# Fewer, larger transfers for x and for the remainders, and the tail product first, in a fused attention and gMLP kernel

## The chip, the cores and the metric

The kernel runs on one core of a Trainium2 chip. The time is device time in microseconds; five runs of the kernel before gave 479.23 to 485.28, with a median of 483.63. A profile is one further reading of such an execution with the hardware profiler on: it lists every instruction with its start, its duration and the engine that it ran on.

## The reference

For 8 batches of 8 heads, with 576 rows of 64 numbers each, the kernel computes an attention in which scores more than `tau` below their row's maximum are dropped, and feeds the joined heads to a gated MLP that mixes rows.

```python
scores = 0.125 * (q @ k.T)                       # per head, 576 x 576
scores = where(scores >= max(scores) - tau, scores, -1e9)
attn = softmax(scores);  x = join_heads(attn @ v)          # 576 x 512 per batch
h = relu(x @ w_in);  u, v = h[:, :512], h[:, 512:]
v_n = (v - mean(v)) / sqrt(var(v) + 1e-6)
out = (u * (w_spatial @ v_n + b_spatial)) @ w_out
```

Inputs and outputs are fp32.

## The kernel before

**Tiling.** Two heads form a pair; there are 32 pairs, four to a batch. A head has 576 rows, that is four blocks of 128 and a remainder of 64. The remainder rows of the two heads of a pair, and of two neighbouring pairs, are put together so that they fill 128 partitions. One *step* computes the scores of one block of one pair for both heads: 128 rows by 2 x 576 columns in fp32. An even pair has four steps (blocks c = 0 to 3). An odd pair has five: first c = 4, the remainder rows of both pairs, and then c = 0 to 3. So there are 144 steps, 18 for each batch. This document calls them s0 to s17:

| steps | pair of the batch | blocks |
|---|---|---|
| s0 to s3 | first | 0, 1, 2, 3 |
| s4 to s8 | second | 4, 0, 1, 2, 3 |
| s9 to s12 | third | 0, 1, 2, 3 |
| s13 to s17 | fourth | 4, 0, 1, 2, 3 |

**One step** (`step`, L606). `scores` (L563) gives the product of q and k in two parts. The first 512 columns of both heads are four independent 64 x 64 products, two heads by two halves of the rows, here called the quadrants (L576). The last 64 columns of both heads are one product over all 128 partitions with a block-diagonal matrix `kd`, here called the tail (L580). The result goes to a PSUM tile of three banks, `s`, of which there are two; a step therefore waits until ScalarE has read the scores of two steps ago. VectorE takes the row maximum (L618). ScalarE computes exponentials from the scores (L641), and VectorE masks them one step later (L599); for blocks 2 and 4 ScalarE does the masking too (L635, L637) and VectorE only shifts the maximum (L622). After the mask of every second block SP issues a DMA transpose of 18 blocks of 128 x 128 (`pT`, L603), or of nine for the remainder rows (`ptr`, L594).

**Jobs.** While VectorE and ScalarE work on a step's scores, PE does up to three jobs that are given out by a list written by hand. In a step, jobs whose result ScalarE takes out of PSUM come first, then those of VectorE; `pv_rest` is last. All jobs share two PSUM banks in turn, so that a job waits until the bank of the job before the last has been read.

- `qk_main` and `qk_rem` (L238, L256) transpose q and k of the next pair in blocks 0, 1 and 2; ScalarE copies them out (L251, L264, L253), and POOL makes `kd` from the copy (L269).
- `pv` (L309) multiplies the transposed weights by v for two blocks of a pair; VectorE divides by the row sums (L302, L304) and writes `xn`. It runs at s3, s4, s7, s8, s12, s13, s16 and s17. The weights used at s4 and s13 belong to the pair before the last.
- `pv_rest` (L336) does the same for the remainder rows of two pairs and writes `xr`. It runs in block 1 of an odd pair, at s6 and s15.
- the gMLP of the batch before: four kinds of jobs, `moe_v`, `moe_u`, `moe_s` and `moe_o`, one in almost every step from step 26 on. `moe_v` begins at s8 of the cycle after the batch.

**x transposed.** The gMLP needs x transposed, `xT`. For most pairs SP issues a DMA transpose of the pair's four blocks as soon as the last are divided (L331), and another of one block for each two pairs' remainders (L352). For pairs 0 to 6, 30 and 31 PE transposes them (`x_pe`, L365), because the list says so.

**Loads.** `load` (L102) brings q, k and v of two pairs at a time, with three main transfers of 512 KB and four smaller ones for the remainder rows: q's and k's go to a fifth block of the tile for q, v's to a fifth block of v's tile, and the odd heads' remainders of v once more to the upper partitions of a tile of their own, `vx`. POOL brings q, k (L137) and v (L157, L161) into the order that PE needs; q's copy carries the fifth block along. One load is issued per step, in the order of a queue. All DMAs but a few at the start and the end are issued by SP, in order, after the transpose of the step's mask. A DMA that writes to a buffer waits on SP until the buffer is free, and everything behind it waits too.

The program below shows the functions that the diff touches.

Of the kernel before, what the change touches and what calls it, by code (L numbers as in the profile page):

```python
# [17 lines left out]
def kernel(  # L18
# [17 lines left out]
    nc = tc.nc  # L36
# [34 lines left out]
    v_ring = [const.tile([P, 11, D + 1], BF16, name=f"v{i}") for i in range(4)]  # L71
    vn_ring = [const.tile([P, 5, 512], BF16, name=f"vn{i}") for i in range(2)]
    ld_ring = [[const.tile([P, 4, n, D], F32, name=f"{t}{i}")
                for t, n in (("ql", 5), ("kl", 4), ("vl", 5))] for i in range(2)]
    vx_ring = [const.tile([P, 2, D], F32, name=f"vx{i}") for i in range(2)]
# [3 lines left out]
    def clear():  # L79
        nc.vector.memset(kd_ring[0], 0.0)  # L80
        nc.gpsimd.memset(ld_ring[0][2][64:128, :, 4, :], 0.0)
        for t in vx_ring:
            nc.gpsimd.memset(t[0:64], 0.0)
        nc.gpsimd.memset(kd_ring[1], 0.0)
        nc.gpsimd.memset(ld_ring[1][2][64:128, :, 4, :], 0.0)
        for t in v_ring:
            nc.vector.memset(t[:, :, D:D + 1], 1.0)
            nc.vector.memset(t[64:128, 4, D:D + 1], 0.0)
            nc.vector.memset(t[0:64, 5, D:D + 1], 0.0)
            nc.vector.memset(t[64:128, 10, D:D + 1], 0.0)  # L90
        for t in vn_ring:
            nc.vector.memset(t[64:128, 4, :], 1.0)
# [9 lines left out]
    def load(i, n, w, eng=nc.sync):  # L102

        b, hp = divmod(i, HP)
        t = ld_ring[i // 2 % 2][w][:, 2 * (i % 2):2 * (i % 2) + 2 * n]
        src = (q, k, v)[w][b, 2 * hp:2 * hp + 2 * n]

        def main():
            eng.dma_start(
                out=t[:, :, 0:4, :],  # L110
                in_=src[:, 0:512, :].rearrange("h (p c) d -> p h (c d)", c=4))

        def rest():

            u = ld_ring[i // 2 % 2][(0, 0, 2)[w]][(slice(0, 64), slice(64, 128), slice(0, 64))[w]]
            eng.dma_start(out=u[:, 2 * (i % 2):2 * (i % 2) + 2 * n, 4, :],
                          in_=src[:, 512:576, :].rearrange("h p d -> p h d"))

        def rest_b():
            nc.sync.dma_start(  # L120
                out=vx_ring[i // 2 % 2][64:128],
                in_=src.rearrange("(j h) s d -> h s j d", h=2)[1, 512:576])
        return [main, rest] + ([rest_b] if w == 2 else [])
# [7 lines left out]
    def shape_qk(i):  # L131

        ts = []
        for w, nm in enumerate(("qn", "kn")):
            n = 5 - w
            t = qkn.tile([P, n, 2, D], F32, name=nm)
# [6 lines left out]
    def shape_first():  # L143

        qn = qkn.tile([P, 5, 2, D], F32, name="qn")
        kn = qkn.tile([P, 4, 2, D], F32, name="kn")
        for to, t, c, copy in ((qn, 0, slice(0, 4), nc.vector.tensor_copy),
                               (kn, 1, slice(0, 4), nc.scalar.copy),
                               (qn, 0, slice(4, 5), nc.gpsimd.tensor_copy)):
            copy(out=to[:, c], in_=ld_ring[0][t][:, 0:2, c].rearrange("p h c d -> p c h d"))  # L150
        nat[0] = [t.rearrange("p c h d -> p c (h d)") for t in (qn, kn)]

    def shape_v(i):
# [5 lines left out]
                        [v_ring[i % 4].ap[0], [6 * (D + 1), 2], [D + 1, 5], [1, D]]),  # L159
            in_=ld_ring[i // 2 % 2][2][:, 2 * j:2 * j + 2])  # L160
        nc.gpsimd.tensor_copy(out=v_ring[i % 4][:, 5, 0:D], in_=vx_ring[i // 2 % 2][:, j, :])  # L161
# [74 lines left out]
    x_on_pe = [j for _, j in x_jobs] + [NPAIR - 2, NPAIR - 1]  # L236

# [18 lines left out]
    def qk_rem(i):  # L256
        hold = {}

        def mm():
            t = hold["t"] = bank()  # L260
            nc.tensor.transpose(out=t[:, 0:P], in_=nat[i][0][:, 4, :], identity=identf)
# [10 lines left out]
    def first():  # L272
# [3 lines left out]
        for t, w, c, at in ([(ts[0], 0, c, c * P) for c in range(5)]  # L276
                            + [(ts[1], 1, c, c * P) for c in range(4)]):
            nc.tensor.transpose(out=t[:, at:at + P], in_=nat[0][w][:, c, :], identity=identf)
# [30 lines left out]
    def pv(i, part):  # L309
# [9 lines left out]
        def ev():  # L319
            if part == 0:  # L320
                xns[i] = xp.tile([P, 4, P], BF16, name="xn")
            xn = xns[i]
            divide(hold["t"], [(slice(0, P), 0, 4,
                                xn[:, 2 * part:2 * part + 2, :].rearrange(
                                    "p c (h d) -> p (c h) d", h=2))])
            if part == 1:
                if hp == 0:
                    xts[b] = xtp.tile([P, 4, 640], BF16, name="xT")
                if i in x_on_pe:
                    return  # L330
                sends.append(lambda: nc.sync.dma_start_transpose(  # L331
                    out=xts[b][:, hp, 0:512].rearrange("p (c s) -> p c s", s=P),
                    in_=xn.rearrange("p c d -> p (c d)")))
        return "dve", mm, ev

    def pv_rest(m):  # L336

        b, hp = divmod(2 * m, HP)
# [7 lines left out]
        def ev():  # L346
            xn = xns["rest", m] = xp.tile([P, P], BF16, name="xr")
# [3 lines left out]
            if 2 * m + 1 < NPAIR - 1:  # L351
                sends.append(lambda: nc.sync.dma_start_transpose(  # L352
                    out=xts[b][:, hp, 512:640], in_=xn))
        return "dve", mm, ev

    def rest_of(b, f):

        return xts[b][:, f - f % 2, 512 + 64 * (f % 2):576 + 64 * (f % 2)]

    def x_pe(i, rest=False):  # L360
# [4 lines left out]
        def mm():  # L365
            t = hold["t"] = bank16()
            for c in range(4):
                nc.tensor.transpose(out=t[:, c * P:(c + 1) * P], in_=xns[i][:, c, :],
                                    identity=identb)
            if rest:  # L370
                nc.tensor.transpose(out=t[:, 512:640], in_=xns["rest", i // 2], identity=identb)

        def ev():
            if not rest:
                nc.scalar.copy(out=xts[b][:, hp, 0:512], in_=hold["t"][:, 0:512])
                return
            nc.scalar.copy(out=xts[b][:, hp, 0:256], in_=hold["t"][:, 0:256])
            nc.vector.tensor_copy(out=xts[b][:, hp, 256:512], in_=hold["t"][:, 256:512])
            nc.vector.tensor_copy(out=xts[b][:, hp - 1, 512:640], in_=hold["t"][:, 512:640])
# [47 lines left out]
    def moe_v(b, c):  # L427
        hold = {}

        def mm():  # L430
# [4 lines left out]
            for f in range(4):  # L435
                nc.tensor.matmul(out=t, lhsT=xts[b][:, f, c * P:(c + 1) * P],  # L436
# [34 lines left out]
    def moe_u(b, f):  # L471
        hold = {}

        def mm():
            t = hold["t"] = bank()
            for m in range(4):
                if f < 4:
                    nc.tensor.matmul(out=t, lhsT=w_in[:, m, f * P:(f + 1) * P],  # L478
                                     rhs=xts[b][:, m, 0:512], start=(m == 0), stop=(m == 3))
# [83 lines left out]
    def scores(i, c):  # L563
# [8 lines left out]
        else:  # L572
            who = tails = [(i - 1 + k, slice(512, 576), halves[k]) for k in range(2)]
        for h in range(2):
# [4 lines left out]
        for n, m, rows in tails:  # L579
            nc.tensor.matmul(out=view(s[rows], 512, [[448, 2], [1, 64]]), lhsT=qks[n][:, 0, m],  # L580
                             rhs=kd_ring[n % 2], start=True, stop=True)
# [84 lines left out]
    def last_gmlp(b):  # L666

        xt, vn = xts[b], vn_ring[b % 2]
# [3 lines left out]
        for c in range(5):  # L672
            t = bank()
            for f in range(4 if c < 4 else 0):
                nc.tensor.matmul(out=t, lhsT=xt[:, f, c * P:(c + 1) * P],
# [130 lines left out]
    with tc.manual_schedule():  # L806
        for w in (0, 1):
            for f in load(0, 1, w, (nc.sync, nc.scalar)[w]):
                f()
# [6 lines left out]
        for w in (0, 1):  # L816
            for f in load(1, 1, w):
                f()
        for f in load(0, 2, 2):
            f()  # L820
# [9 lines left out]
        for g, (i, c) in enumerate(steps):  # L830
# [4 lines left out]
            if c == 0 and i % 2 and i + 3 < NPAIR or g == 0:  # L835
                for w in range(3):
                    queue.extend(load(i + (3 if g else 2), 2, w))
# [81 lines left out]
```

## Time and profile before

| | |
|---|---|
| median of five runs | 483.63 us |
| lowest, highest | 479.23, 485.28 us |
| profiled execution: device time | 484.91 us |
| its span, first to last instruction | 483.1 us |
| mean granted TensorE clock | 0.992 |
| VectorE, row maximum (L618): 144 of | 1.353 us |
| VectorE, mask (L599): 91 of | 1.474 us |
| SP, transposes issued: pT, xT from xn, xT from xr, ptr | 64, 23, 15, 13 |
| SP, instructions | 272 |
| DMA engines busy, 0 to 115, 115 to 430, 430 to 483 us | 0.90, 0.95, 0.48 |

In the profile "PE" is the matmul stream and "PEld" the loading of weights, which may run beside it. Every fp32 matmul of the program appears as two[...]. In a row of a group or of the timeline, `out<-in` are the program's tiles; in brackets stands how long the engine was idle before, and what ended that. The chain of work that ended last is followed back from the last instruction, at each step to what released it. "SPq" is the time for which SP's queue was held by issuing a DMA, not the time of the transfer; "landing" is when the transfer's completion was seen.

### The profile page before, as it was taken

How to read it: one execution, taken by the hardware profiler on the slowest of the kernel's cores; microseconds unless marked ns; L12 is line 12 of the kernel's file. 1: busy time of each engine (PE TensorE's matmuls, PEld its weight loads, DVE VectorE, ACT ScalarE, POOL GpSimd, SP SyncE). 2: the span in 40 equal slices, each digit the busy share in tenths (PEclk: the TensorE clock that was granted, in tenths of full speed). 3: DMA queues.
4: the chain of work that ended last, by engine and by line, in shares of the span. 5: the costliest groups of instructions: out<-in, count | busy, mean ns of one | idle time of the engine just before them, and what ended most of it. 6: DMA issues, size and time to landing. Idle time of an engine off the chain costs nothing.

```text
span 483.1 us, 10876 instructions
## 1 busy us (share of the span) xinstructions
PE 446.1 (92%) x4153; PEld 226.8 (47%) x4203; DVE 412.8 (85%) x563; ACT 390.8 (81%) x677; POOL 227.2 (47%) x403
## 2 busy tenths in 40 slices
PE   8788888889899999999999999999997999999995
PEld 5244444444544445454544545454543445445542
DVE  3889898989889997999889998999986898899573
ACT  3889998999879798888979798788978689797351
POOL 3453335795438553574427643575416444153021
PEclk9899999999999999999999999999999999999999
DMA  8879899969999899899999899899999989568523
GB/s 231 218 176 202 196 211 206 223 142 190 196 193 187 166 216 224 204 157 191 217 215 173 178 193 229 189 187 188 182 178 199 187 163 211 133 114 125 148 81 116
DMA packets 226131, 88.55 MB, mean 183 GB/s; under 512 B 196896, under 2 KB 221600, under 8 KB 226080
## 3 DMA queue, kind: packets, MB, share of 16 engines
q1 hardware_dynamic: 225424, 86.98, 87.7%
q8 instruction: 33, 0.54, 0.5%
q0 software_dynamic: 160, 0.52, 0.3%
q10 hardware_dynamic: 496, 0.36, 0.2%
q14 instruction: 18, 0.15, 0.1%
HBM read 33.31 MB, written 9.44 MB: 88 GB/s over the span
## 4 chain that ended last, share of the span: by engine, by line
PE 47%; DVE 24%; ACT 20%; issue 6%; DMA 2%; POOL 0%; POOLq 0%; ACTq 0%; DVEq 0%
PE s L576 14%; DVE negm L618 11%; DVE p L599 8%; PE s L580 6%; ACT e L641 5%; ACT e L635 5%; PE f L295 4%; PE f L478 3%; PE f L246 3%; PE f L537 2%; ACT p L637 2%; DMA pT<-p 2%; PE f L508 2%; PE f L290 2%; ACT vrel L446 2%
## 5 line engine op out<-in xcount | busy, mean ns | idle before, releaser
L618 DVE TENSOR_REDUCE negm<-s 128x2 f32<-128x1152 f32 x144 | 194.9, 1353 | 33.2 <-PE s L580 31.7
L576 PE MATMUL s<-qkT 64*64 64x512 f32 x1152 | 159.5, 624 | 14.3 <-ACT e L641 8.3
L599 DVE SCALAR_TENSOR_TENSOR p<-e,ctau 128x1152 bf16<-128x1152 f32 x91 | 134.1, 1474 | 1.2 <-ACT e L641 1.2
L641 ACT ACTIVATE e<-s,negm 128x576 f32<-128x576 f32 x182 | 124.9, 741 | 7.2 <-DVE negm L618 6.7
L580 PEld LDWEIGHTS s<-kd,qkT 128*128 128x128 f32 (+1 forms) x320 | 41.7, 179 | 119.2 <-issue 107.0
L635 ACT ACTIVATE e<-s,negm 128x576 f32<-128x576 f32 x106 | 72.9, 742 | 16.2 <-DVE negm L622 10.9
L269 POOL COPY kd<-qkT 64x64 f32<-64x64 f32 x62 | 26.9, 434 | 101.8 <-ACT qkT L264 100.0
L580 PE MATMUL s<-kd,qkT 128*128 128x128 f32 (+1 forms) x320 | 70.2, 323 | 0.0
L576 PEld LDWEIGHTS s<-qkT 64*64 64x64 f32 x1152 | 30.2, 132 | 46.8 <-ACT e L641 18.3
L454 POOL TENSOR_SCALAR nmean<-sm 128x1 f32<-128x1 f32 (+1 forms) x35 | 16.6, 473 | 71.2 <-ACT vrel L446 59.5
L295 PEld LDWEIGHTS <-pT 128*128 128x128 bf16 x1024 | 41.8, 97 | 9.1 <-issue 5.8
L295 PE MATMUL f<-v,pT 128*128 128x65 bf16 x992 | 44.9, 194 | 0.0
L637 ACT ACTIVATE p<-e 128x1152 bf16<-128x1152 f32 x37 | 43.1, 1164 | 1.2
L137 POOL COPY qn<-ql 128x640 f32<-128x640 f32 x31 | 32.6, 1052 | 14.2 <-DMA ql<-in_k_dram 10.2
L290 PE MATMUL f<-v,pT 128*128 128x130 bf16 x124 | 27.2, 219 | 7.8 <-DMA pT<-p 4.5
L508 PE MATMUL f<-wsT,vn 128*128 128x512 bf16 x119 | 31.3, 385 | 0.3
L466 POOL TENSOR_SCALAR vn<-vrel,rs,nm 128x512 bf16<-128x512 f32 (+1 forms) x34 | 29.7, 874 | 3.7
L251 ACT ACTIVATE qkT<-f 128x512 f32<-128x512 f32 x31 | 18.3, 590 | 14.4 <-PE f L246 14.0
L157 POOL CAST v<-vl 128x640 bf16<-128x640 f32 x32 | 28.6, 894 | 1.5 <-DMA vl<-in_v_dram 1.5
L478 PE MATMUL f<-xT,w_in 128*128 128x512 bf16 x97 | 27.6, 379 | 1.7 <-DVE xn L304 0.8
L436 PE MATMUL f<-w_in,xT 128*128 128x512 bf16 x102 | 28.3, 379 | 0.5
L253 ACT COPY qkT<-f 128x512 f32<-128x512 f32 x31 | 18.3, 589 | 12.6 <-PE f L246 12.0
(168 smaller groups left out, 647.9 us busy)
## 6 DMA issues: line engine op xcount, KB each, us to landing
vl<-in_v_dram SPq DMA_DIRECT2D x16, 512.0 KB, 4.7
ql<-in_q_dram SPq DMA_DIRECT2D x15, 512.0 KB, 4.9
kl<-in_k_dram SPq DMA_DIRECT2D x15, 512.0 KB, 4.5
out_dram<-oo SPq DMA_DIRECT2D x10, 512.0 KB, 3.6
uT<-in_moe_w_in_dram SPq DMA_DIRECT2D x3, 512.0 KB, 6.2
uT<-in_moe_w_spatial_dram SPq DMA_DIRECT2D x2, 576.0 KB, 5.9
vl<-in_v_dram SPq DMA_DIRECT2D x16, 64.0 KB, 4.4
pT<-p SPq DMA_TRANSPOSE x64, 5.4
```

The costliest lines, as they stand in the source:

```text
L137: nc.gpsimd.tensor_copy(out=t, in_=ld_ring[i // 2 % 2][w][:, 2 * (i % 2):2 * (i % 2) + 2].rearrange("p h c d -> p c h d"))
L290: nc.tensor.matmul(out=t[:, at:at + 130], lhsT=pt[:, 4, :], rhs=vt[:, 4:6, :].rearrange("p b d -> p (b d)"), start=True, stop=False)
L295: nc.tensor.matmul(out=t[:, at + 65 * h:at + 65 * h + 65], lhsT=pt[:, 5 * h + j, :], rhs=vt[:, 6 * h + j, :], start=False, stop=(h == 1 an ...
L478: nc.tensor.matmul(out=t, lhsT=w_in[:, m, f * P:(f + 1) * P], rhs=xts[b][:, m, 0:512], start=(m == 0), stop=(m == 3))
L508: nc.tensor.matmul(out=t, lhsT=vn[:, c, f * P:(f + 1) * P], rhs=wsT[:, c, 0:512], start=(c == 0), stop=(c == 4))
L576: nc.tensor.matmul(out=s[rows, 1024 * h:1024 * h + 512], lhsT=qks[n][halves[h], 0, m], rhs=qks[n][halves[h], 1, 0:512], start=True, stop=True)
L580: nc.tensor.matmul(out=view(s[rows], 512, [[448, 2], [1, 64]]), lhsT=qks[n][:, 0, m], rhs=kd_ring[n % 2], start=True, stop=True)
L599: nc.vector.scalar_tensor_tensor(out=pt[:, c % 2, :], in0=ef, scalar=ctau, in1=ef, op0=ALU.is_ge, op1=ALU.mult)
L618: nc.vector.tensor_reduce(out=nm, in_=s, axis=AX.X, op=ALU.max, negate=True)
L635: nc.scalar.activation(out=e[:, h, :], in_=s[:, h, :], func=ACT.Prelu, bias=nm[:, h:h + 1], scale=by, alpha=1e30)
L637: nc.scalar.activation(out=pr_ring[i // 2 % 2] if c == 4 else p_ring[2 * (i % 2) + c // 2][:, c % 2], in_=e.rearrange("p h s -> p (h s)"), ...
L641: nc.scalar.activation(out=e[:, h, :], in_=s[:, h, :], func=ACT.Exp, bias=nm[:, h:h + 1])
```

## The change

There are four parts.

1. *x.* `xn` becomes one tile of nine blocks for two pairs: four blocks of each and the block of their remainder rows. `xT` takes the same order. Once the second pair's last blocks are divided, SP issues one transpose of nine blocks (five, if PE transposes the first pair's). For the first three of these tiles, whose pairs PE transposes, the remainder block is still sent alone.
2. *Order of `pv_rest`.* So that the remainder block is ready by then, `pv_rest` runs in block 1 of the even pair that follows, at s1 and s10, five steps earlier than before. For the first three it stays where it was.
3. *Remainder loads.* The remainder rows of q and k are loaded once per batch for all eight heads, into a tile of their own from which PE transposes them directly; those of v are loaded once per batch, the even heads' to the lower and the odd heads' to the upper partitions. POOL's copy of q no longer carries a fifth block; v's remainders are copied by two casts of 64 partitions. Some clearing at the start goes.
4. *Scores.* In `scores` the tail is issued ahead of the quadrants.

```diff
-    v_ring = [const.tile([P, 11, D + 1], BF16, name=f"v{i}") for i in range(4)]
+    v_ring = [const.tile([P, 10, D + 1], BF16, name=f"v{i}") for i in range(4)]
...
-                for t, n in (("ql", 5), ("kl", 4), ("vl", 5))] for i in range(2)]
-    vx_ring = [const.tile([P, 2, D], F32, name=f"vx{i}") for i in range(2)]
+                for t, n in (("ql", 4), ("kl", 4), ("vl", 4))] for i in range(2)]
+    rest_ring = [const.tile([P, H, D], F32, name=f"rl{i}") for i in range(2)]
+    vx_ring = [const.tile([P, HP, D], F32, name=f"vx{i}") for i in range(2)]
...
+    def load_rest(b, w, h0=0, h1=H, eng=nc.sync):
+
+        if w < 2:
+            return lambda: eng.dma_start(
+                out=rest_ring[b % 2][64 * w:64 * w + 64, h0:h1, :],
+                in_=(q, k)[w][b, h0:h1, 512:576, :].rearrange("h p d -> p h d"))
+        return lambda: eng.dma_start(
+            out=vx_ring[b % 2][64 * (w - 2):64 * (w - 2) + 64],
+            in_=v[b].rearrange("(j h) s d -> h s j d", h=2)[w - 2, 512:576])
...
+    def nat_rest(i):
+
+        return rest_ring[i // HP % 2][:, 2 * (i % HP):2 * (i % HP) + 2, :].rearrange(
+            "p h d -> p (h d)")
...
-        nc.gpsimd.tensor_copy(out=v_ring[i % 4][:, 5, 0:D], in_=vx_ring[i // 2 % 2][:, j, :])
+        for h in range(2):
+            hs = slice(64 * h, 64 * h + 64)
+            nc.gpsimd.tensor_copy(out=v_ring[i % 4][hs, 4 + h, 0:D],
+                                  in_=vx_ring[i // HP % 2][hs, i % HP, :])
...
+    rest_late = (0, 1, 2)
...
-            nc.tensor.transpose(out=t[:, 0:P], in_=nat[i][0][:, 4, :], identity=identf)
+            nc.tensor.transpose(out=t[:, 0:P], in_=nat_rest(i), identity=identf)
...
-                    xts[b] = xtp.tile([P, 4, 640], BF16, name="xT")
-                if i in x_on_pe:
-                    return
-                sends.append(lambda: nc.sync.dma_start_transpose(
-                    out=xts[b][:, hp, 0:512].rearrange("p (c s) -> p c s", s=P),
-                    in_=xn.rearrange("p c d -> p (c d)")))
+                    xts[b] = xtp.tile([P, 2, 9 * P], BF16, name="xT")
+            elif i not in x_on_pe and i % 2:
+                n0 = 4 if i - 1 in x_on_pe else 0
+                send_x(i // 2, n0, 9)
...
+    def send_x(m, n0, n1):
+
+        xn, to = xns[m], xts[m // 2][:, m % 2, n0 * P:n1 * P]
+        sends.append(lambda: nc.sync.dma_start_transpose(
+            out=to.rearrange("p (c s) -> p c s", s=P),
+            in_=xn[:, n0:n1, :].rearrange("p c d -> p (c d)")))
...
-            if 2 * m + 1 < NPAIR - 1:
-                sends.append(lambda: nc.sync.dma_start_transpose(
-                    out=xts[b][:, hp, 512:640], in_=xn))
+            if m in rest_late:
+                send_x(m, 8, 9)
...
-            nc.vector.tensor_copy(out=xts[b][:, hp, 256:512], in_=hold["t"][:, 256:512])
-            nc.vector.tensor_copy(out=xts[b][:, hp - 1, 512:640], in_=hold["t"][:, 512:640])
+            nc.vector.tensor_copy(out=xts[b][:, hp // 2, 768:1152], in_=hold["t"][:, 256:640])
...
+        for n, m, rows in tails:
+            nc.tensor.matmul(out=view(s[rows], 512, [[448, 2], [1, 64]]), lhsT=qks[n][:, 0, m],
+                             rhs=kd_ring[n % 2], start=True, stop=True)
         for h in range(2):
             for n, m, rows in who:
                 nc.tensor.matmul(out=s[rows, 1024 * h:1024 * h + 512],
                                  lhsT=qks[n][halves[h], 0, m], rhs=qks[n][halves[h], 1, 0:512],
                                  start=True, stop=True)
-        for n, m, rows in tails:
-            nc.tensor.matmul(out=view(s[rows], 512, [[448, 2], [1, 64]]), lhsT=qks[n][:, 0, m],
-                             rhs=kd_ring[n % 2], start=True, stop=True)
...
+                n = i + (3 if g else 2)
                 for w in range(3):
-                    queue.extend(load(i + (3 if g else 2), 2, w))
+                    queue.append(load(n, 2, w))
+                    if n % HP == 0:
+                        queue += [load_rest(n // HP, j) for j in ((0,), (1,), (2, 3))[w]]
...
-            if i % 2 and i > 1 and c == 1:
+            if i > 1 and c == 1 and i % 2 == (i // 2 - 1 in rest_late):
                 small_ones = [pv_rest(i // 2 - 1)]
```

## The prediction

> **What bounds the kernel now.** I read the engine shares first, then the chain of work that ended last, because no engine is full.
>
> ```profile
> PE 446.1 (92%) x4153; PEld 226.8 (47%) x4203; DVE 412.8 (85%) x563; ACT 390.8 (81%) x677; POOL 227.2 (47%) x403
> ...
> PE 47%; DVE 24%; ACT 20%; issue 6%; DMA 2%; POOL 0%; POOLq 0%; ACTq 0%; DVEq 0%
> ```
>
> Three engines take turns: TensorE (PE) holds half of the chain, VectorE and ScalarE the rest. POOL is not on it, DMA 2%. So I need the turns, from the chain in order of time. From about 120 us on one cycle of 18 steps (s0 to s17) repeats, e.g. from 218.6 to 273.5 us: 54.9 us. Within it the chain runs over PE from s16 to s6 (212 to 237 us), then turns:
>
> ```profile
> 235.78 1.02 PE s L576 x8
> 236.80 0.43 PE s L580 x2
> 237.29 1.24 issue
> 238.53 1.41 DVE p L599
> 239.94 0.10 DVE r L302
> 240.07 0.28 DVE xr L304
> 240.37 0.29 DVE xr L304
> 240.69 1.37 DVE negm L618
> ...
> 264.93 1.26 ACT e L641 x2
> 266.19 0.17 ACT qkT L264
> 266.36 0.04 issue
> 266.40 0.22 PE f L290
> ```
>
> Both places where `pv_rest` stands are on the chain: at s6 with its divisions on VectorE (r, xr), at s15 with its matmuls (L290, waiting for a PSUM bank that L264 frees). Between them, from s9 to s13, VectorE has no gap (249.8 to 260.5 us), then ScalarE none until 266.4.
>
> The timeline of one step gives the price of the two score products.
>
> ```profile
> 242.11 0.21 PEld L576 LDWEIGHTS s<-qkT 64*64 64x64 f32 x8
> 242.11 1.09 PE L576 MATMUL s<-qkT 64*64 64x512 f32 x8
> ...
> 243.13 0.30 PEld L580 LDWEIGHTS s<-kd,qkT 128*128 128x128 f32 x2 [0.81 <-issue]
> 243.13 0.49 PE L580 MATMUL s<-kd,qkT 128*128 128x128 f32 x2
> ...
> 243.46 1.03 PE L537 MATMUL f<-w_o,gT 128*128 128x512 bf16 x3
> ```
>
> The quadrants take 1.02 us until the tail's weights may load (0.81 us of it the loader waits, though nothing is shown that it waits for), the next job's matmul starts 1.35 us in, and the scores are complete at 243.62, 1.51 us in. The DMA part shows once, late in the run, where a transposed block of weights came too late:
>
> ```profile
> 371.99 0.10 PEld L290 LDWEIGHTS <-pT 128*128 128x128 bf16 x1 [3.60 <-DMA pT<-p]
> ```
>
> Its DMA was issued at 362.41 and landed at 371.95, 9.5 us later, the longest of all 64 (median 5.4). At this position (s13) the same transpose landed only 0.3 to 2.8 us ahead of its use in the cycles before and after.
>
> [...] start to start, a 512-column bf16 matmul is followed by another after 0.216 us, by a quadrant after 0.309; a 65-column one after 0.032 and 0.125. Each time 0.093 us more. [...] fp32 transposes follow each other at 0.109 us with the load hidden, the first tail pass after the drain takes 0.213. [...] a transpose of one block holds the queue 1.22 us, of four 1.28, of nine 1.27.
>
> **The order of the score products.** Before, from the end of the previous job's stream: drain 0.093, quadrants 0.50 to their last pass, 0.427 for it and 0.092 drain, tail 0.213, 0.111 to the next job: 1.44 us; scores complete at 1.60. After: tail 0.109 (its load now under the previous job), 0.107 plus drain 0.093, quadrants 0.50, then 0.519 and the next job's exposed load E: 1.33 + E; scores complete at 0.109 + 0.200 + 0.50 + 0.589 = 1.40. E is 0.107 for an fp32 transpose (blocks 0 to 2) and about 0.01 for bf16 (a bf16 weight load after a wait delays its matmul by that much in the trace). Where the previous job is a `pv`, its last matmul (0.032) hides only part of the tail's load: add 0.075. Where the scores wait for a free buffer (34 of 144 steps), the load is not hidden and the sums are 1.50 against 1.51 for ready. So PE itself changes by -0.10 to +0.08 us a step, near zero over a cycle, and the maximum can start 0.1 to 0.2 us earlier, which counts only where VectorE is idle then: 60 steps, most of them inside a stretch that is PE's anyway, or waiting for a buffer. One thing isn't shown: a change from bf16 to fp32 without a change of tile. fp32 to bf16 without one costs nothing (0.109). I take 0; bounds 0 and 0.093 us a step. Below zero there is no reason: nothing is removed.
>
> **`pv_rest` five steps earlier** (12 of 16; those of pairs 0 to 5 stay, the last is in the closing part). From s6 to s1, six times. At s1 its bank is freed by L264, which ScalarE does at 224.39, after e of s0; so its 0.62 us of matmuls end near 225.1 and the scores of s2, at 224.28 now, start 0.8 later. s2 to s6 are PE's alone, so s6 is 0.8 later; its scores are ready 0.2 earlier than that: +0.6. Then the 0.70 us of PE and 0.66 of VectorE at s6 are gone; what is late next is p of s5 on VectorE: the maximum of s7 begins about 0.2 us earlier than now. Net -0.2. From s15 to s10, six times: at s10 it adds 0.66 to VectorE's gapless stretch and 0.62 to PE, where L508 of s11 now waits for the bank that xr frees: by s13 about +1.0. It reaches e of s14, which ends near 267.2 instead of 266.19. At s15 the matmuls that held PE until 267.02 are gone, but the scores of s16 need the buffer that e of s14 frees: 267.2. What is late next is that wait: +0.2 with the tail's load in it, +0.3. Together +0.2 us a cycle (from -0.4, if s10 finds a gap, to +1.5, if nothing is given back at s15), six cycles: +1.2 us (-2.4 to +9).
>
> **Fewer DMAs.** Transposes of x on SP go from 38 (23 of four blocks, 15 of one) to 15 (11 of nine, one of five, three of one): 23 fewer by about 1.25 us. Remainder loads go from 66 to 34 (one of each number on ScalarE's queue): 32 fewer by 0.62. SP loses 29 + 20 = 49 us of issue. Blocks moved stay 107, and the bytes fall by 16 x 32 KB, so the DMA engines (95% busy from 115 to 430 us) gain little. SP is off the chain: it mostly waits for p, and the merged transpose goes out where the pair's last went before, four steps before its first reader, so it costs nothing; if that cover were gone, one landing (3.3 us) a batch. What it changes is the queue ahead of the tight pT at s13: one 1.22 us transpose less in front, so loads start earlier, against 64 KB more in each remainder load of q and k and 32 KB more for v in that half of the cycle. I expect a stall such as that of 3.6 us to shrink to 1.5: -2 us (0 to -5.2, the sum of the weight loader's three waits for such a block in the trace, at 44.8, 55.3 and 372 us).
>
> **The rest.** POOL copies 128 fewer columns of q per pair (1052 against 648 ns for k's 512: about 12 us over 31) and adds 32 casts of v's remainders; its cover is its own idle half, so 0; bare it would be some 3 us saved. At the start the tail runs while L284 still copies (the quadrants now wait 1.01 us for it): -0.5 us. At the end two VectorE copies (0.51 us) become one: -0.1.
>
> **Sum.** The profiled execution took 484.91 us (span 483.1 plus 1.8 around it): 0 + 1.2 - 2 - 0.5 - 0.1 = -1.4, so 483.5. It is 1.3 us above the median of the five; the same difference on the median 483.63 gives 482.2 us.
>
> **Rivals.** (1) It is faster: all three stalls on DMA go (-5.2) and the earlier maximum shortens the turn from PE to VectorE in each cycle (0.2 at s6 and at s9, seven cycles, -2.8): 476. For it: the slack at s13 is small in every cycle. Against: DMA is 2% of the chain. (2) It is slower: bf16 to fp32 drains like a change of tile. Then every PE-paced step with a bf16 job ahead pays 0.093 in the gap between job and tail; 114 steps follow a job without a wait, some 86 of them on PE's part of the chain: +8, so 490. It decides from 0.06 us a step (1% over 86 steps). Against: nothing in the trace shows it; its drains are all explained by the tile. (3) The moved `pv_rest` is not paid back at s15 (+1.5 a cycle in all, +9): 490; against: it is on the chain there now. (4) The change does nothing: 483.6.
>
> **Chances.** A measurement tells about 1% (4.8 us) from no change. Forecast, near nothing: 0.50, with (4) 0.03: within 1%, 0.53. (1) 0.27, faster. (2) 0.11 and (3) 0.09, slower: 0.20. The range leaves out some tenth at each end: just below (1), 475, to (2) and (3), 490.
>
> **What would show it.** In the trace after: the quadrants' load right behind the tail and 0.2 us from it; the wait of 0.81 in front of the job's load; tail start to scores ready 1.4 us; scores of s2 0.8 us later within the cycle; no r, xr at s6 and s15; a cycle of 54.9 to 55.2 us; 217 instructions on SP for 272; no stall at s13 over 2 us. A gap of 0.2 between job and tail, or a cycle over 55.7 or under 54.2, makes the prediction wrong.

## The result and the profile after

The changed kernel takes 483.86 us (median; the kernel before takes 481.10 us in the same comparison). The ratio is 1.0068, interval 1.0054 to 1.0082, so the change is about 3.3 us slower. The ratio is taken over fast executions alone, without those that lie over 1.5% above the fastest of their kernel, so it is not the quotient of the two medians. The prediction said 1.4 us faster. The time lies inside the range that it gave, but the direction is wrong, and by more than the measurement's uncertainty.

The page of the kernel after: shares of the engines, and the chain of work that ended last by engine.

```profile
PE 443.0 (92%) x4146; PEld 228.1 (47%) x4203; DVE 409.8 (85%) x558; ACT 389.2 (81%) x677; POOL 214.7 (45%) x430
...
PE 45%; ACT 28%; DVE 11%; DMA 8%; issue 5%; POOL 1%; SPq 0%; POOLq 0%; ACTq 0%; DVEq 0%
```

TensorE and VectorE are each busy 3 us less, and the kernel is slower. Neither of the two has much less to do. The profile of before has two stretches of 3.4 us, from 21.6 and from 373.1 us, in which the granted clock was 0.50, and the profile of the change has none until 478 us; that TensorE worked some 3.4 us longer for it (half of the two stretches) is an estimate from these figures. VectorE's 3 us lie in the durations of two operations (13.7 us before and 11.9 now for the small one behind the maximum, 134.1 and 132.3 for the mask `p`). Both last longer in places where a copy, a cast or `vn` of POOL started before them and still runs; the experiments take this up. On the chain VectorE falls from 24% to 11%, ScalarE rises from 20% to 28% and DMA from 2% to 8%. Three things are to be read from the views below.

The order of the score products does what it should. The timeline of one step in the kernel after, around the same job (`w_o`, now L546) as the step shown before:

```profile
241.42 0.30 PEld L584 LDWEIGHTS s<-kd,qkT 128*128 128x128 f32 x2
241.45 0.46 PE L584 MATMUL s<-kd,qkT 128*128 128x128 f32 x2
241.84 0.21 PEld L588 LDWEIGHTS s<-qkT 64*64 64x64 f32 x8
241.84 1.09 PE L588 MATMUL s<-qkT 64*64 64x512 f32 x8
...
242.86 0.55 PEld L546 LDWEIGHTS <-gT 128*128 128x128 bf16 x4 [0.81 <-issue]
```

The quadrants' weights load right behind the tail, and the wait of 0.81 us now stands in front of the job's load. From the tail's start to the end of the scores it takes 1.48 us here, behind a `pv`, and 1.40 behind a 512-column job. From a 512-column bf16 job to the fp32 tail the trace has 0.216 us from start to start, as between two such bf16 matmuls: without a change of tile nothing like the 0.093 us that the prediction calls a drain is added between bf16 and fp32.

Second, new waits on DMA (view of the waits; columns: engine, tile and line, what it waited for, us in all, times, longest):

```profile
PEld L289 <- DMA pT<-p: 4.9, 5, 2.0
POOL w_o L178 <- DMA o<-in_moe_w_out_dram: 3.8, 2, 2.4
PEld L445 <- DMA xT<-xn: 2.0, 4, 0.6
PE f L433 <- POOL w_o L178: 1.7, 1, 1.7
```

The first line was 5.2 us in three waits before; the third was 0.4 us in one, and there was no wait of TensorE for `w_o`. The chain around the first `moe_v` of a batch shows the merged transpose (start, us, piece):

```profile
238.12 0.44 SPq L558
238.56 0.06 issue
238.62 5.75 DMA xT<-xn
```

Nine blocks are sent at 238.62 and land at 244.37, 5.75 us later (at this place four blocks took 3.8 in the trace of before); the weight loader of L445 stands 0.57 us for them at 244.41. Size alone does not set the 5.75 us: at the other place of a batch, nine blocks landed in about 3.4 us in five batches.

Third, the cycle of 18 steps is longer. From the trace, start of s0 to start of s0, in the three cycles from step 72 on, counted from 0 (in brackets a cycle in which the weight loader waits 1.4 us or more for `pT`; 'L631 in two' is explained with its run):

| kernel | cycles, us | time, ratio to before |
|---|---|---|
| before | 54.90, 54.89, (59.87) | 1 |
| before, profiled again | (57.05), 54.88, (58.90) | |
| loads merged | (58.23), 54.88, 54.88 | 0.9985 |
| loads, s6 moved | 54.90, 54.88, 54.89 | 0.9988 |
| loads, both moved | 55.53, 55.52, 55.52 | 1.0067 |
| loads, tail first | 56.05, (56.17), (56.17) | 1.0066 |
| loads, tail, both moved | 55.42, 55.43, 55.43 | 1.0040 |
| after | 55.68, (56.56), 55.67 | 1.0068 |
| loads, L631 in two | 55.38, 55.38, 55.37 | 0.9998 |
| loads, both moved, in two | 55.37, 55.37, 55.37 | 0.9994 |
| loads, tail, in two | 55.21, 55.21, (55.38) | 0.9973 |
| loads, tail, s6 moved, in two | 55.09, 55.09, 55.08 | 0.9946 |
| after, L631 in two | 55.53, 55.41, 55.53 | 1.0016 |

The change's cycle is 0.78 us longer where 0.2 was predicted. The first profile of before was also an execution above the median: it carries the stall at 372 us, and its third cycle is 5.0 us longer than the other two. The wait for `pT` is only 3.6 us of that; right behind it lies the second stretch with a granted clock of 0.50. The waits in the cycles of 58.90 and 58.23 us have such a stretch of 3.4 us behind them too. With the loads and the tail first, the cycles with a wait have none, and are only 0.12 us longer than the one without.

### The profile page after: what moved, and what is told of

The parts are those of the page before. It is cut to its first block, busy times and chain, and to the rows that moved or that the text cites. A ratio compares the mean times of both kernels' runs of the same rounds, so it can differ in the third digit from the quotient of the medians.

```text
span 481.5 us, 10795 instructions
## 1 busy us (share of the span) xinstructions
PE 443.0 (92%) x4146; PEld 228.1 (47%) x4203; DVE 409.8 (85%) x558; ACT 389.2 (81%) x677; POOL 214.7 (45%) x430
## 4 chain that ended last, share of the span: by engine, by line
PE 45%; ACT 28%; DVE 11%; DMA 8%; issue 5%; POOL 1%; SPq 0%; POOLq 0%; ACTq 0%; DVEq 0%
PE s L588 13%; ACT e L650 7%; ACT e L644 6%; DVE negm L627 6%; PE s L584 4%; DVE p L608 4%; PE f L294 4%; DMA pT<-p 3%; PE f L243 3%; PE f L517 3%; PE f L546 3%; ACT p L646 3%; DMA xT<-xn 2%; PE f L445 2%; ACT sq L469 2%
## 5 line engine op out<-in xcount | busy, mean ns | idle before, releaser
L588 PE MATMUL s<-qkT 64*64 64x512 f32 x1152 | 156.8, 615 | 0.0
L608 DVE SCALAR_TENSOR_TENSOR p<-e,ctau 128x1152 bf16<-128x1152 f32 x91 | 132.3, 1454 | 1.2 <-ACT e L650 1.2
L584 PE MATMUL s<-kd,qkT 128*128 128x128 f32 (+1 forms) x320 | 63.8, 302 | 13.9 <-ACT e L650 9.1
L266 POOL COPY kd<-qkT 64x64 f32<-64x64 f32 x62 | 28.3, 456 | 98.6 <-ACT qkT L261 97.1
L584 PEld LDWEIGHTS s<-kd,qkT 128*128 128x128 f32 (+1 forms) x320 | 44.8, 179 | 33.8 <-ACT e L650 15.9
L463 POOL TENSOR_SCALAR nmean<-sm 128x1 f32<-128x1 f32 (+1 forms) x35 | 9.6, 274 | 80.1 <-ACT vrel L455 80.0
L303 DVE TENSOR_TENSOR xn<-f,r 128x256 bf16<-128x256 f32 (+1 forms) x94 | 35.6, 378 | 2.9
L517 PE MATMUL f<-wsT,vn 128*128 128x512 bf16 x119 | 30.8, 379 | 3.6 <-DVE xn L303 3.3
L445 PE MATMUL f<-w_in,xT 128*128 128x512 bf16 x96 | 28.6, 381 | 1.0
L127 POOL COPY qn<-ql 128x512 f32<-128x512 f32 x31 | 24.3, 785 | 9.1 <-DMA ql<-in_q_dram 7.7
L455 ACT ACTIVATE vrel<-f 128x512 f32<-128x512 f32 (+1 forms) x34 | 20.1, 591 | 10.1 <-PE f L445 5.5
```

Of the source, the lines that this page charges most:

```text
L303: nc.vector.tensor_tensor(out=dst, in0=o[ps, g0:g1, 0:64], in1=r[ps, g0:g1].unsqueeze(2).broadcast_to([ps.stop - ps.start, g1 - g0, 64]), ...
L445: nc.tensor.matmul(out=t, lhsT=x_of(b, f, slice(c * P, (c + 1) * P)), rhs=w_in[:, f, 512:1024], start=(f == 0), stop=(f == 3))
L517: nc.tensor.matmul(out=t, lhsT=vn[:, c, f * P:(f + 1) * P], rhs=wsT[:, c, 0:512], start=(c == 0), stop=(c == 4))
L588: nc.tensor.matmul(out=s[rows, 1024 * h:1024 * h + 512], lhsT=qks[n][halves[h], 0, m], rhs=qks[n][halves[h], 1, 0:512], start=True, stop=True)
L608: nc.vector.scalar_tensor_tensor(out=pt[:, c % 2, :], in0=ef, scalar=ctau, in1=ef, op0=ALU.is_ge, op1=ALU.mult)
```

## The experiments

All kernels are made from the changed one by undoing parts; line numbers are its own (L631 is L622 of the kernel before, the small VectorE operation that scales the negated maximum and adds tau; L608 is `p`). The four parts are: remainder loads merged; x transposes merged; `pv_rest` moved; tail first.

### The parts, undone one after the other

**Loads alone.** x goes out in fours, `pv_rest` and its block from its old place, the quadrants are first:

```
-    rest_late = (0, 1, 2)
+    rest_late = tuple(range(NPAIR // 2 - 1))
...
-            elif i not in x_on_pe and i % 2:
-                n0 = 4 if i - 1 in x_on_pe else 0
-                send_x(i // 2, n0, 9)
+            elif i not in x_on_pe:
+                n0 = 4 * (i % 2)
+                send_x(i // 2, n0, n0 + 4)
```

and in `scores` the loop over `tails` stands behind that over `who` again.

> The merged remainder loads alone; the x transposes, pv_rest and the order of the score products as before. Theory (the moved pv_rest and the merged x transposes make the loss, some 0.8 us per cycle; what is gained, about 3 us before the 40th step, comes from the start, the tail first and the loads): 1 to 2 us faster than before, ratio 0.996 to 0.999. Rival (the larger remainder loads hold up the DMA queue, so that other transfers land late): 1 to 3 us slower than before, with waits on pT or on the weights in the chain.

Measured: 0.9985, 0.9961 to 1.0009. The likeliest figure is 0.7 us faster, but that is no difference that shows; the cycle is that of before. TensorE still waits 3.0 us for `pT`, in another cycle.

**Loads and the tail first** (the same with the two loops in `scores` as in the change):

> The merged remainder loads and the tail product first; the x transposes and pv_rest as before. Theory: 2.5 to 4 us faster than before, ratio 0.992 to 0.995, with a cycle of 54.9 us as before or less. Rival (the tail first itself costs, by the loads that it leaves uncovered, some 0.05 us a step): slower than the run with the loads alone by 2 us or more, with a cycle of 55.4 us.

Measured: 1.0066, 1.0033 to 1.0100. My theory falls here: the tail first alone costs 3.9 us against the loads alone (uncertain by 2.0), and the cycle without a stall grows by 1.2 us, from 54.88 to 56.05. The rival's size is right; whether its reason is, the next group tells.

**The change without the merge into nine** (an even pair's four blocks are sent alone, the odd pair's four with the remainder):

```
-            elif i not in x_on_pe and i % 2:
-                n0 = 4 if i - 1 in x_on_pe else 0
-                send_x(i // 2, n0, 9)
+            elif i not in x_on_pe:
+                n0 = 4 * (i % 2)
+                send_x(i // 2, n0, 9 if i % 2 else 4)
```

> The change with each even pair's four blocks of x sent on their own, at the place of before, and the odd pair's four with the remainder block: only the merge into nine is undone. Theory: the moved pv_rest costs 0.6 us a cycle, 3.5 us in all, and the merge up to 2 us, by the wait for xT in front of the first moe_v of a batch: 481 to 483 us where the change has 484, and no wait for xT. If the move is the whole of the loss: 484, as the change. If the merge is the whole of it: 478 to 479.

Measured: 1.0040, 1.0022 to 1.0059, and no wait for xT. The merge into nine thus costs about 1.3 us (1.0040 to 1.0068, uncertain by 1.1). The cycles say the same: without the merge a cycle is 0.25 us shorter (55.43 against 55.68), all of it at s9, behind the wait for xT. But this kernel is not slower than loads and tail: moving `pv_rest` on top of the tail first takes nothing, against my theory.

**The change with the quadrants first:**

> The change with the quadrants first again: only the order of the score products is undone. Theory (the order gives little in a cycle, and about 1 us at the start): 0.5 to 2 us slower than the change, 484.8 to 486. Rival (the order is the loss): 2 us or more faster than the change, 482 or less.

Measured: 1.0075, 1.0046 to 1.0104: no different from the change within the uncertainty. So the order costs 3.9 us where `pv_rest` is at s15 and nothing that shows where it is at s10. The parts don't add up; something is shared between them.

**Loads and the moved `pv_rest`** (x in four and five as above, quadrants first):

> The merged remainder loads and pv_rest at its new place, x sent in two parts (four blocks, then four and the remainder), the quadrants first. Theory (the move costs about 0.55 us in each of six cycles, whatever stands first in the score products): 3 us slower than the run with the loads alone, 482 to 483.5 us, and a cycle of 55.4 us. Rival (the move costs only with the tail first): within 1 us of the loads alone, 479 to 480.5.

Measured: 1.0067, 1.0043 to 1.0091; cycle 55.52. The move costs 3.9 us on its own, as expected.

**The same with only s6 moved to s1**; s15 stays:

```
-    rest_late = (0, 1, 2)
+    rest_late = (0, 1, 2, 4, 6, 8, 10, 12, 14)
```

(the blocks of those pairs are sent from `pv_rest`).

> The merged loads and the quadrants first, with pv_rest moved from s6 to s1 only; at s15 it stays. Theory (the move from s6 to s1 is paid back by s9, the one from s15 to s10 loses 0.6 us a cycle): as the run with the loads alone, 479 to 480.3 us, where the run with both moves had 482.1; cycles of 54.9 us. Rival (both halves lose): 481 us or more.

Measured: 0.9988, 0.9971 to 1.0005; cycle 54.89. Moving s6 to s1 is free, moving s15 to s10 is the whole loss of the move: 0.64 us a cycle and 3.8 us in all.

### What the tail first and s10 share

In the trace of loads and tail, VectorE's time differs where its work does not: 414.1 us busy against 409.5. The row of L631 is the one that grew. First the row of loads and tail, then that of loads alone (columns: count, busy us, mean ns of one, idle before it):

```profile
L631 DVE TENSOR_SCALAR negm<-negm 128x2 f32<-128x2 f32 x53 | 15.8, 298 | 1.8
```

```profile
L631 DVE TENSOR_SCALAR negm<-negm 128x2 f32<-128x2 f32 x53 | 11.8, 223 | 1.8
```

This operation on two elements a partition takes 0.17 us where no operation of POOL on 128x512 has started before it, as at 311.61 below. The timeline of s10 to s12 in loads alone, VectorE and POOL:

```profile
308.90 1.41 DVE L608 SCALAR_TENSOR_TENSOR p<-e,ctau 128x1152 bf16<-128x1152 f32 x1
308.95 1.41 POOL L463 TENSOR_SCALAR nmean<-sm 128x1 f32<-128x1 f32 x1 [0.87 <-ACT vrel L455]
...
311.61 0.17 DVE L631 TENSOR_SCALAR negm<-negm 128x2 f32<-128x2 f32 x1
311.64 0.78 POOL L475 TENSOR_SCALAR vn<-vrel,rs,nm 128x512 bf16<-128x512 f32 x1
...
312.28 1.41 DVE L608 SCALAR_TENSOR_TENSOR p<-e,ctau 128x1152 bf16<-128x1152 f32 x1
312.37 1.80 POOL L127 COPY qn<-ql 128x512 f32<-128x512 f32 x1
```

and the same stretch of a cycle in loads and tail:

```profile
251.76 1.41 DVE L608 SCALAR_TENSOR_TENSOR p<-e,ctau 128x1152 bf16<-128x1152 f32 x1
251.77 0.19 POOL L463 TENSOR_SCALAR nmean<-sm 128x1 f32<-128x1 f32 x1 [0.82 <-ACT vrel L455]
...
254.23 0.77 POOL L475 TENSOR_SCALAR vn<-vrel,rs,nm 128x512 bf16<-128x512 f32 x1
254.47 0.55 DVE L631 TENSOR_SCALAR negm<-negm 128x2 f32<-128x2 f32 x1
254.95 0.61 POOL L127 COPY qn<-ql 128x512 f32<-128x512 f32 x1
255.53 1.79 DVE L608 SCALAR_TENSOR_TENSOR p<-e,ctau 128x1152 bf16<-128x1152 f32 x1
```

In the first, POOL's `nmean` comes 0.05 us behind `p` and lasts 1.41 instead of 0.19 us, until `p` ends; POOL's chain is then late, L631 comes just ahead of `vn`, and the next `p` just ahead of POOL's copy, which lasts 1.80 instead of 0.61. In the second, ScalarE's result (`vrel`) comes some 0.04 us earlier relative to `p`, `nmean` is not held (by the trace it starts 0.01 us behind `p`, too close to say which came first), and from there POOL is ahead: L631 waits 0.38 us behind `vn`, `p` 0.38 behind the copies. At s13 L631 waits 0.44 again (0.61 at 260.43). That is 1.2 us of VectorE's gapless stretch, as much as the cycle grew by. That the 0.04 us start all this is read from the two timelines and not tested by itself; that L631's wait costs time is tested next. In two of these pairs the operation that started second lasts longer, until just after the first has ended: L631 at 254.47 ends at 255.02 and `vn`, which started before it, at 255.00; `nmean` at 308.95 ends at 310.36 and `p`, which started before it, at 310.31. What the two engines have in common there is not shown; in what follows, a wait of VectorE for POOL is the time by which L631 lasts longer than its 0.17 us at 311.61, or `p` than its 1.41.

**L631 in two.** The same kernel; the operation is written for one element at a time. That it then does not wait for POOL was the author's guess:

```
-                nc.vector.tensor_scalar(out=nm, in0=nm, scalar1=by, scalar2=float(tau),
-                                        op0=ALU.mult, op1=ALU.add)
+                for h in range(2):
+                    nc.vector.tensor_scalar(out=nm[:, h:h + 1], in0=nm[:, h:h + 1], scalar1=by,
+                                            scalar2=float(tau), op0=ALU.mult, op1=ALU.add)
```

> The loads merged and the tail first, pv_rest as before (the run of 483.4 us), with one thing changed: the small VectorE operation behind the maximum (L631, 128x2) is written as two of one element each[...]. Theory (in that run POOL's copies come just ahead of L631 and of p at s11 and s13, and VectorE waits 0.3 us and more each time; that is the loss of the tail first): L631's 6.9 us of waiting go, 2 to 4 us faster, 479.5 to 481.5. Rival (the loss is the weight loads of the tail that are not covered): no change, or 0.5 us slower by the added instructions.

Measured: 0.9973, 0.9960 to 0.9987: 4.5 us faster than with L631 whole (uncertain by 1.7), more than expected, and faster than before. The cycle without a stall falls by 0.84 us, from 56.05 to 55.21. Its row and the place (now L632), beside the same `vn`:

```profile
L632 DVE TENSOR_SCALAR negm<-negm 128x1 f32<-128x1 f32 x106 | 11.4, 149 | 1.8
```

```profile
253.05 0.77 POOL L475 TENSOR_SCALAR vn<-vrel,rs,nm 128x512 bf16<-128x512 f32 x1
253.29 0.22 DVE L632 TENSOR_SCALAR negm<-negm 128x1 f32<-128x1 f32 x2
```

Started 0.24 us into `vn`, as at 254.47 above, the two together take 0.22 us instead of 0.55; why one element does not wait is not shown. So most of what the tail first costs is L631's wait for POOL and not the weight loads: the rival that had the size right had the wrong reason. Of the cycle's 1.17 us, 0.33 remain; `p` still waits at s11 and s15.

**Loads alone with L631 in two:**

> The merged loads alone, with the small operation behind the maximum written as two of one element each, the quadrants first. It tells what the tail first is worth[...]. Theory (the tail first is worth what the trace's start shows, some 0.5 us, and nothing in a cycle): 478.0 to 479.0 us, 0 to 1 us slower than the same with the tail first (478.07). If the tail first costs after all: below 477.5.

Measured: 0.9998, 0.9977 to 1.0018. Against 0.9973 with the tail first, the order is worth about 1.2 us, uncertain by as much. Here the split itself gains nothing: its cycle is 0.5 us longer than with L631 whole, since now `p` at s11 and s15 waits for POOL (2.2 and 1.3 us over all cycles). That the times are the same is in part less waiting for `pT` in its trace (1.4 us for 3.0); the rest is not explained.

**Loads and the moved `pv_rest` with L631 in two:**

> The merged loads and the moved pv_rest, the quadrants first (the run of 482.1 us), with L631 in two of one element each. It splits the loss of the move from s15 to s10. Theory (most of it is TensorE's and the bank's: 0.6 us of matmuls and 0.7 us of the wait for the bank at s11, of which 0.9 comes back at s16[...]): 480.5 to 481.5, 1 us better. Rival[...]: 479.3 or less.

Measured: 0.9994, 0.9972 to 1.0015, 3.5 us (uncertain by 1.6) less than with L631 whole, and as fast as without the move. By the times the rival, that L631's waits are the loss as with the tail first, is nearer: without L631's wait the move costs nothing that shows. By the cycles the theory is: only 0.15 us of 0.64 went (55.52 to 55.37), in each of the three; of the 2.7 us between the two traces 1.5 lie ahead of step 72 and 0.7 behind step 126. Times and cycles disagree here, and what the split gains outside the cycles is not explained. Within a cycle the trace of loads and moved `pv_rest` shows the parts (the stretch from s10 on, then s16):

```profile
306.27 0.22 PE L289 MATMUL f<-v,ptr 128*128 128x130 bf16 x1
306.33 0.42 PE L294 MATMUL f<-v,ptr 128*128 128x65 bf16 x8
306.67 1.09 PE L585 MATMUL s<-qkT 64*64 64x512 f32 x8
...
309.13 1.25 PE L517 MATMUL f<-wsT,vn 128*128 128x512 bf16 x5 [0.52 <-DVE xn L303]
...
310.41 0.61 POOL L127 COPY qn<-ql 128x512 f32<-128x512 f32 x1
310.50 0.54 DVE L631 TENSOR_SCALAR negm<-negm 128x2 f32<-128x2 f32 x1
...
325.02 0.61 POOL L127 COPY kn<-kl 128x512 f32<-128x512 f32 x1
325.32 0.34 DVE L631 TENSOR_SCALAR negm<-negm 128x2 f32<-128x2 f32 x1
```

Against the kernel in which s15 stays, `pv_rest` at s10 puts the scores of s11 0.62 us later, and L517 then waits for the bank that the division frees, which puts s12 at 1.31 behind. At s16 0.87 us come back, which leaves 0.44. L631 waits for POOL's copies, 0.37 us at s11 and 0.17 at s16. With L631 in two no step from s11 to s17 starts more than 0.04 us earlier, so the wait at s11 costs nothing there; the next s0 starts 0.15 us earlier. In a cycle, then, 0.44 of the 0.64 us are TensorE's and the bank's, and the rest comes behind s16, where L631's wait accounts for 0.15.

The tail first and the move to s10 share these waits between VectorE and POOL, which fits that their costs don't add up. The row of L631 with the tail first and both moved:

```profile
L631 DVE TENSOR_SCALAR negm<-negm 128x2 f32<-128x2 f32 x53 | 12.6, 239 | 1.8
```

It was 15.8 us with the tail first alone. The waits at s11 and s13 are 0.10 and 0.04 us here, where they were 0.38 and 0.44: the moved `pv_rest` shifts VectorE against POOL once more and takes away most of what the tail first costs.

**The change with L631 in two:**

> The change, with L631 in two of one element each. Theory ([...]the moved pv_rest's own 0.5 us a cycle stays): 1 to 3 us faster than the change, 480.5 to 482.5, and still slower than before. [...]

Measured: 1.0016, 0.9997 to 1.0035: 2.5 us faster than the change (uncertain by 1.1). That most of the 3.3 us is L631's waits doesn't follow. By the cycles without a stall only 0.15 of 0.78 us goes, again between s17 and the next s0, and over the whole trace L631 waits no longer in the change than in before (busy 11.9 us against 13.7). Of the 4.6 us between the two traces some 3 are a late `w_o` and a stall on `pT` that only the change's trace has.

### DMA

**`w_o` earlier.** In the change the last load of `w_o` lands late once (POOL's cast, then TensorE):

```profile
163.53 1.33 POOL L178 CAST w_o<-o 128x512 bf16<-128x512 f32 x1 [2.42 <-DMA o<-in_moe_w_out_dram]
164.91 0.38 PE L433 MATMUL f<-w_o,gT 128*64 128x512 bf16 x1 [1.71 <-POOL w_o L178]
```

```
-                   ((36, 41, 46, 51), load_w_o), ((39, 44, 49, 54), shape_w_o)):
+                   ((36, 40, 44, 48), load_w_o), ((39, 43, 47, 51), shape_w_o)):
```

> The change with the last two loads of w_o two and three steps earlier and their casts with them. Theory (in the change the last one lands at 163.1 us, POOL's cast and TensorE wait for it, 2.2 us lost at one place): 1.5 to 2.2 us faster than the change, 481.5 to 482.5. Rival (the stall belongs to that one execution, or is given back within the next steps): within 0.5 us of the change.

Measured: 1.0052, 1.0033 to 1.0071. TensorE's wait is gone from its trace, but of the 2.2 us only some 0.8 show in the times, and not beyond the uncertainty: inconclusive.

**Before, profiled again:**

> The kernel before, profiled a second time, to tell what in its first profile is steady. Theory (the 1.6 us that all kernels with merged loads were ahead by the sixth step are the loads' doing): the second profile reaches the sixth step at 24.5 us again. Rival (that was a stretch of half clock in the one execution): it reaches it at about 23 us. In both, cycles of 54.9 us; the stall of 3.6 us at 372 us is not expected in the same place.

Measured: the sixth step at 22.80 us, against 24.54 in the first profile (steps counted from 0), so the 1.6 us are not the loads' doing. They were lost in the first step: its eight 512-column matmuls (L576) take 1.98 us in the first profile and 1.09 in the second, so TensorE ran there at little more than half its pace. The stretch with a granted clock of 0.50 near 20 us is in both. The stall at 372 us was there again (cycle of 58.90), against what I expected, and one of 2.2 us two cycles earlier. This execution took 483.71 us, 4.5 us over the median of 479.17 in its group: both profiles of before seem to show more stall than a usual execution has.

**x merged, with the old place of `pv_rest`** (eight blocks, and the remainder's from its own place), loads, tail, L631 in two:

> The kernel of 478.07 us (loads merged, tail first, L631 in two) with x sent per two pairs, eight blocks at once and the remainder's block from where pv_rest stands. Theory (the merge costs up to 0.3 us a batch, by the wait of the first moe_v for xT): 0.5 to 2 us slower, 478.6 to 480. Rival (fewer, larger transposes free the queue, pT lands earlier): 477.5 or less.

Measured: 0.9996, 0.9973 to 1.0019, so 1.1 us slower than unmerged, uncertain by 1.3. Its trace has no wait for xT: with only eight blocks and nothing moved, it is inconclusive. The wait for xT was there in all four traces with nine blocks (2.0 to 3.0 us in 4 or 5 waits).

### A version that beats both

Loads, tail first, L631 in two, and only s6 moved to s1; and the one without the move but with `w_o` earlier:

> The kernel of 478.07 us (loads merged, tail first, L631 in two) with pv_rest moved from s6 to s1 only and x in four blocks or five. Theory (that half of the move is paid back, with the tail first 0.2 us more than that a cycle): 477 to 478.2. Rival: any move costs, 479 or more.

> The kernel of 478.07 us with the last two loads of w_o and their casts two and three steps earlier. Theory (there the last w_o lands late for POOL alone, TensorE doesn't wait for it): 477.5 to 478.3, no difference that shows. If the wait reaches TensorE in some executions: 477 or less.

Measured: the first 0.9946, 0.9926 to 0.9965 (2.6 us faster than before, and 1.3 faster than without the move, uncertain by 1.1), with the shortest cycle of those with the tail first (55.09). The second 0.9981, 0.9962 to 1.0001: earlier weight loads add nothing that shows.

## Why the prediction was wrong, by its own steps

- **The order of the products, taken as 0.** Its working held: no drain between bf16 and fp32 (0.216 us), 1.40 us from the tail's start to the scores, the quadrants 0.20 behind the tail, so rival (2) falls. The effect did not: 3.9 us slower where `pv_rest` stays at s15, about 1.3 faster (uncertain by 1.5) where it is moved. The step that failed is "the maximum can start 0.1 to 0.2 us earlier, which counts only where VectorE is idle then". It also counts where it changes which of VectorE and POOL starts first and so which of them waits: 1.2 us a cycle with the loads and the tail first, of which 0.84 goes with L631 in two.
- **`pv_rest`, s6 to s1, -0.2 a cycle.** The places were right, the gain was smaller: 0.0 with the quadrants first (0.86 us later at s2, given back at s7 and s9), and -0.10 by s9 with the tail first on both sides.
- **`pv_rest`, s15 to s10, +0.3 a cycle.** This is the term that was mis-sized most: 0.64 in the trace, 3.8 us in the times instead of 1.8. The places were right (s11 +0.62, then the wait of L517 for the bank), but they sum to 1.31 by s12 instead of 1.0, the return at s16 is 0.87, and 0.19 more comes behind s16, of which L631's wait for POOL is 0.15. The two terms were also added wrongly: -0.2 and +0.3 make +0.1 a cycle and not +0.2, +0.6 us and not +1.2, which would have put the forecast still further down. Rival (3) said +1.5 a cycle with nothing paid back: too much.
- **Fewer DMAs, -2.** The merged loads bring 0.7 us, no more than their uncertainty. The sum credited a stall of the profiled execution to the change, while that execution, and the second, lay 3.8 and 4.5 us above the medians that they are compared with. And "four steps before its first reader, so it costs nothing" failed: nine blocks land up to 5.75 us after their issue and the reader waits, 2.0 us in the trace and about 1.3 in the times. The other bound, "one landing (3.3 us) a batch", was far too wide.
- **The rest.** "its cover is its own idle half, so 0" for POOL's casts looked only at whether POOL has time, not at whom it holds up. The end (-0.1) is too small to tell, and so is the start (-0.5): the first scores begin between 7.2 and 8.2 us in all the traces, without order.

Taken one after the other, from before to the change, the times say: loads -0.7, s6 to s1 +0.1, s15 to s10 +3.8, tail first on top of that -1.3, x merged +1.3. That they sum to the measured loss is no test, since each is the difference of two neighbours on that way, and in another order the tail first costs 3.9 us and the move nothing that shows. Against the prediction's terms the DMAs (loads and merge) came out 2.6 us worse, s15 to s10 2.0 and s6 to s1 1.3 worse, and the order 1.3 better. Rival (1) had no base: the stalls it took away were mostly not in the median.

Of the signs named beforehand, the load behind the tail, the wait in front of the job, 1.4 us, s2 0.8 later, no division at s6 and s15 and 55 instructions fewer on SP came true, and the longest stall at s13 was 2.0 us, just at its limit; a cycle of 54.9 to 55.2 did not (55.68, near the 55.7 that was to disprove it).

## What to carry to other kernels

Where VectorE had no gap here and POOL worked beside it, a shift of some 0.04 us in ScalarE's result seems to have decided which of the two waited for the other, and the waits that follow add up to 1.2 us a cycle; so look at the durations of short VectorE operations in the groups (L631: 0.17 us alone, 0.55 behind `vn`) before blaming the edit, and look where in the cycle the waits lie: the change has fewer of them than before (L631 busy 11.9 us against 13.7) and is slower. Writing the tiny operation in two is worth a trial: it gained 4.5 us where L631's waits lay in the gapless stretch, and with the loads alone it gained nothing and made the cycle 0.5 us longer. Don't credit a change with a stall of one profiled execution that lies above the median. A job moved from one place to another gave back only what the next wait in line allowed (0.87 us at s16 of the 1.31 by s12), so both places count, with the banks that they share and the engines that they hold up.

## What the runs showed of the hardware

A VectorE operation of 128x2 elements, begun 0.24 us into a POOL operation of 0.77, took 0.55 us instead of 0.17, and two of 128x1, begun at the same place in such an operation, took 0.22 us together; a POOL operation of 0.19 us took 1.41 when it started 0.05 us behind the mask `p` on VectorE, itself 1.41 us. From bf16 to fp32 without a change of tile TensorE lost nothing (0.216 us, as between two bf16 matmuls). What stays open is the stalls on `pT`: 0.7 to 8.4 us of the weight loader's time from kernel to kernel, in other cycles each time, with no rule that these runs show.
